# Second MLP layer as one product of 512 columns and one of 256, with channel 128 of the column DFT on GpSimd and two weight decodes moved

## The chip, the cores and the metric

The kernel runs on one core of a Trainium2 chip. The metric is device time in microseconds (us) of one execution. The text calls the engines TensorE (PE in the rows, PEld its weight loads), VectorE (DVE), ScalarE (ACT), GpSimd (POOL) and SyncE (SP), which issues the DMAs.

## The reference

The input is x, 2 x 3136 x 256 in float32. Three blocks follow one another.

```python
X = np.fft.rfft(x, axis=1)                       # spectral mixing
Yr = X.real @ w_r - X.imag @ w_i + b_r
Yi = X.real @ w_i + X.imag @ w_r + b_i
y = np.fft.irfft(soft_threshold(Yr, 0.01) + 1j * soft_threshold(Yi, 0.01), n=3136, axis=1)

xn = (y - mean) / sqrt(var + 1e-6) * g_ln        # MLP 1, weights in float64
z = y + np.maximum(xn @ w_ch1, 0) @ w_ch2        # 256 -> 1024 -> 256

u = z + np.real(np.fft.fft(np.fft.fft(z, axis=1), axis=2))
un = (u - mean) / sqrt(var + 1e-6)               # MLP 2, other weights in float64
out = u + np.maximum(un @ w_ch1, 0) @ w_ch2
```

## The kernel before, in words

**Stages.** The DFT over 3136 is done as 49 x 64 with matrices in two steps. Stages 1 to 3 are the mixing block, up to about 165 us. From there on the two MLPs fill the program: 13 chunks of MLP 1 (`mlp1[0]` to `mlp1[12]`), then 13 of MLP 2 (`mlp2[0]` to `mlp2[12]`), each chunk of up to four tiles of 128 rows. Stage 4 (`Stage98`) is the first step of the DFT over z. It is woven into MLP 1's chunks 7 to 10 for batch 0 and into MLP 2's chunks 0 to 3 for batch 1.

**Precision.** A matrix that needs more than one pass is held as two float32r parts, a high one (h) and a low one (l). A product is then three products: h by h, h by l, l by h. `mm3` (lines 214 to 216) and `mm3r` (lines 220 to 222) issue them.

**One MLP chunk.** `Chunk.prep` computes the layer norm, `Chunk.trans` transposes on TensorE (line 607) and splits into h and l (ScalarE line 612 or 202, VectorE line 613 or 210). `Chunk.l1` runs the first layer, eight slices `f` of 128 hidden units: six matmuls of 512 columns into a PSUM tile `psa` (three buffers), then ScalarE writes the ReLU's high part (line 631) and VectorE its low part (line 632), which frees `psa`. `Chunk.l2` runs the second layer tile by tile: 8 slices by three matmuls of 256 columns into `psb` (two buffers), then VectorE adds the residual `y` (line 649) and SyncE stores (line 657). There are 98 tiles in all, 49 for each MLP.

**Weights.** `load_mlp` brings each MLP's weights in eight pieces of float64 and VectorE decodes a piece to h and l in eight instructions (`decode64`, lines 506 to 514). They lie in `r3a` (MLP 1) and `r2b` (MLP 2), h and l in separate halves of the tile (`w_views`). `MLP2_AT` says after which slice of which MLP 1 chunk MLP 2's pieces are decoded.

**Stage 4.** For each group of two columns `Stage98.split` folds channel c with channel 256 - c on GpSimd (lines 360 to 362), ScalarE writes the high part `s` (line 202), GpSimd the low part (line 210), TensorE does three matmuls (`psc<-s`), ScalarE copies out (`o`), GpSimd puts channel 128 in (line 405), SyncE stores. Channel 128, which has no partner, goes apart: `middle` loads it for all columns (line 373, tile `m`), `middle2` splits it (`mhl`), multiplies it and copies it to `mid`.

**What sets the order.** Each engine takes its instructions in the order of the built program, and SyncE its DMAs. A scheduler makes that order: it lists what can run by a timeline of its own, so a change in one place moves instructions elsewhere. `tc.issue_after`, the tables above and buffer counts bind it.

Of the kernel before, what the change touches and what calls it, by code (L numbers as in the profile page):

```python
# [11 lines left out]
I32 = mybir.dt.int32  # L12
# [10 lines left out]
STAGE3_AT = (0,) * 16 + (3, 3, 3, 3, 3, 1)  # L23
CONST_AT = (0, 0, 1, 2, 2, 3, 4, 5, 6, 8)
MLP1_AT = (5, 8, 10, 12, 13, 14, 15, 18)
MLP2_AT = ((4, 6), (5, 2), (5, 6), (6, 2), (6, 6), (7, 3), (9, 3), (10, 6))
STAGE3_END = 3
STAGE3_MLP = ((0, 0), (0, 1), (0, 2), (0, 3), (1, 0), (1, 1), (1, 2), (1, 3),
              (2, 0), (2, 1), (2, 2), (2, 3), (3, 0))
# [18 lines left out]
ALU = mybir.AluOpType  # L48
# [5 lines left out]
D = 256  # L54
NQ = 98
# [5 lines left out]
NF = DFF // 128  # L61
# [101 lines left out]
def fourier_moe_kernel(ctx, tc, x, w_r, w_i, b_r, b_i, g_ln, w11, w12, w21, w22,  # L163
                       t_ca, t_cam, t_cim, t_cb, t_ci, t_cb0, t_ci0, t_cd, t_ident, out):
    nc = tc.nc
# [9 lines left out]
    def psum(tag):  # L175
        return pp.tile([128, 512], F32, tag="ps" + tag, name="ps" + tag, bufs=ps_bufs[tag])
# [20 lines left out]
    def oslot():  # L197
        return wk.tile([128, 4, D], F32, tag="o", name="o", bufs=2)


    def a_copy(o, i, scale=1.0):
        nc.scalar.activation(out=o, in_=i, func=AF.Copy, scale=scale)

    def v_copy(o, i):
        nc.vector.tensor_copy(o, i)
# [3 lines left out]
    def sub(eng, o, a, b):  # L209
        ins = eng.tensor_tensor(out=o, in0=a, in1=b, op=ALU.subtract)  # L210
        mark["pool" if eng is nc.gpsimd else "dve"] = getattr(ins, "ins", ins)

    def mm3(ps, lh, ll, rh, rl, first, last):
        nc.tensor.matmul(out=ps, lhsT=lh, rhs=rh, start=first, stop=False)  # L214
        nc.tensor.matmul(out=ps, lhsT=lh, rhs=rl, start=False, stop=False)  # L215
        nc.tensor.matmul(out=ps, lhsT=ll, rhs=rh, start=False, stop=last)  # L216
# [117 lines left out]
    class Stage98:  # L334
# [40 lines left out]

        def middle2(self):
            t, hl = self.mid_in
            v_copy(hl[:, 0], t)
            sub(nc.vector, hl[:, 1], t, hl[:, 0])
            ps = psum(self.tag)  # L380
            mm3(ps[0:NQ, 0:32], cs_h, cs_l, hl[:, 0], hl[:, 1], True, True)
            self.mid = wk.tile([NQ, 32], F32, tag="mid", name="mid", bufs=1)
            v_copy(self.mid, ps[0:NQ, 0:32])

        def start(self):
            self.middle()
# [106 lines left out]
    def load64(src3, tag):  # L493

        s64 = wk.tile([128, 512], I64, tag=tag, name="s64", bufs=2)
        o = s64 if len(src3.shape) == 2 else s64.rearrange("p (f c) -> p f c", f=src3.shape[1])
        sp.dma_start(out=o, in_=src3)
        return s64

    def decode64(s64, dh, dl, t1, t2):  # L500


        w, low = s64.bitcast(I32)[:, 1::2], s64.bitcast(U32)[:, 0::2]
        t1f, t2f = t1.bitcast(F32), t2.bitcast(F32)
        v = nc.vector
        v.tensor_scalar(out=t1, in0=w, scalar1=3, scalar2=0x3FFFF000,
                        op0=ALU.logical_shift_left, op1=ALU.bitwise_and)
        v.scalar_tensor_tensor(out=t1, in0=w, scalar=-0x40000000, in1=t1, op0=ALU.bitwise_and, op1=ALU.bitwise_or)
        v.tensor_scalar(out=t2, in0=w, scalar1=20, scalar2=0x7FF, op0=ALU.logical_shift_right, op1=ALU.bitwise_and)
        v.scalar_tensor_tensor(out=dh, in0=t2, scalar=896.0, in1=t1f, op0=ALU.is_gt, op1=ALU.mult)  # L510
        v.tensor_scalar(out=t2, in0=w, scalar1=0x1FF, scalar2=None, op0=ALU.bitwise_and)
        v.scalar_tensor_tensor(out=t2f, in0=low, scalar=2.0 ** -32, in1=t2, op0=ALU.mult, op1=ALU.add)
        v.tensor_scalar(out=t1, in0=dh.bitcast(I32), scalar1=-0x800000, scalar2=None, op0=ALU.bitwise_and)
        v.scalar_tensor_tensor(out=dl, in0=t2f, scalar=2.0 ** -20, in1=t1f, op0=ALU.mult, op1=ALU.mult)

    def load_mlp(w1, w2, r, tag, two):

        srcs, raw = [], {}  # L520
        for i in range(4):
            c, h = divmod(i, 2)
            srcs.append((w1[c * 128:(c + 1) * 128, h * 512:(h + 1) * 512], i * 512))
        for i in range(4):
            srcs.append((w2[i * 256:(i + 1) * 256, :].rearrange("(f p) c -> p f c", p=128), 2048 + i * 512))

        def ask(k):
            if k < 8 and k not in raw:
                raw[k] = load64(srcs[k][0], tag)

        def piece(k):
            def f():
                ask(k)
                if two:
                    ask(k + 1)
                    t1, t2 = (wk.tile([128, 512], I32, tag="t98", name="t64", bufs=TB) for _ in range(2))
                else:
                    t = wk.tile([128, 2, 512], I32, tag="stg", name="t64", bufs=SB)
                    t1, t2 = t[:, 0, :], t[:, 1, :]
                o = srcs[k][1]  # L540
                decode64(raw[k], r[:, 0, o:o + 512], r[:, 1, o:o + 512], t1, t2)
            return f

        return [lambda: ask(0)] + [piece(k) for k in range(8)]

    def w_views(r):
        return ([r[:, i, 0:2048].rearrange("p (k f) -> p k f", k=2) for i in range(2)],
                [r[:, i, 2048:].rearrange("p (f c) -> p f c", f=NF) for i in range(2)])

    class Chunk:  # L550

# [85 lines left out]
            self.h.append((h, l))  # L637

        def l2(self, i):
            _, (w2h, w2l) = self.wv  # L640
            if i == 0:
                self.o = oslot()
            ps = psum("b")
            ts_ = slice(i * 128, (i + 1) * 128)
            with tc.issue_after(self.last):
                for f in range(NF):
                    h, l = self.h[f]
                    mm3(ps[:, 0:D], h[:, ts_], l[:, ts_], w2h[:, f, :], w2l[:, f, :], f == 0, f == NF - 1)
            nc.vector.tensor_tensor(out=self.o[:, i, :], in0=ps[:, 0:D], in1=self.y[:, i, :], op=ALU.add)  # L649

        def store(self, last):

# [159 lines left out]

    r3 = cp.tile([128, 2, 4096], F32R, tag="r3", name="r3a")
    wv1 = w_views(r3)
    mlp1_w = load_mlp(w11, w12, r3, "o", False)[1:]
    todo = {}
# [84 lines left out]
    inv1 = lambda: inv[1].step()  # L901
    r2b = cp.tile([128, 2, 4096], F32R, tag="u1", name="r2b")
    wv2 = w_views(r2b)
    plan2 = [[((0, 4 * i + 2), (0, 4 * i + 1)), ((0, 4 * i + 4), (0, 4 * i + 3))] for i in range(6)]
    plan2 += [[((1, 2), (1, 1)), ((0, 0), (1, 0))]]
# [12 lines left out]
    def after(k, i, f):  # L918

        def g():  # L920
            with tc.issue_after(mlp1[k].rest[i]):
                f()
        return g
# [8 lines left out]
    def hook(k, part, i, f):  # L932
        hooks.setdefault((k, part, i), []).append(f)

    mlp2_w = load_mlp(w21, w22, r2b, "stg", True)
    hook(4, "l1", 2, mlp2_w[0])
    for (k, i), f in zip(MLP2_AT, mlp2_w[1:]):
        hook(k, "l1", i, after(k, i, f))
# [42 lines left out]
```

## Time and profile before

| what | value |
|---|---|
| runs | 838.01, 839.77, 841.67 us; median 839.77 |
| the profiled execution's own time | 835.99 us |
| its span, first to last instruction | 834.2 us |
| mean granted TensorE clock | 0.998 |
| busy share: TensorE, VectorE, ScalarE, GpSimd | 98%, 60%, 37%, 17% |
| DMA | 71.66 MB, mean 86 GB/s |

Busy shares are sums over the span. A matmul's duration in the rows includes its way through the array and overlaps the next one, so the pace of a stream of matmuls is read from the distance between starts, not from durations. In a row of the timeline, the brackets give the idle time of the engine just before it and what ended it.

### The profile page before, as it was taken

What the parts mean: (1) busy time and instruction counts of PE and PEld (TensorE: products, weight loads), DVE (VectorE), ACT (ScalarE), POOL (GpSimd) and SP (SyncE); (2) the same over time, 40 slices, a digit from 0 to 9 for tenths busy, and PEclk for the clock granted to TensorE, in tenths of its full rate; (3) what the DMA queues carried; (4) which work ended last, traced back from release to release, by engine and by line L of the source; (5) the groups of instructions that cost most, each with busy time, mean ns of one, the idle gap of its engine ahead of it and who ended that gap; (6) DMA issues with size and microseconds to landing.
All of it is one profiled execution on the core that took longest, in us unless ns stands there. A gap on an engine that the chain in (4) does not pass through costs nothing.

```text
span 834.2 us, 13615 instructions
## 1 busy us (share of the span) xinstructions
PE 813.7 (98%) x5240; PEld 716.1 (86%) x5240; DVE 499.3 (60%) x1152; ACT 312.3 (37%) x627; POOL 141.1 (17%) x198
## 2 busy tenths in 40 slices
PE   9999999999999999989999998999999999999997
PEld 3888977868888999959799998899899999999996
DVE  6579995475565578754755345625545566545652
ACT  1322356354343222364553225455532233322221
POOL 0212221320000000097410004345400000000000
PEclk9999999999999999999999999999999999999999
DMA  8642200711014321453133113343232122210001
GB/s 230 215 139 72 76 1 1 244 67 51 23 29 158 127 77 67 116 171 121 56 105 101 64 49 77 109 139 103 86 96 86 46 62 59 70 51 25 18 19 30
DMA packets 48180, 71.66 MB, mean 86 GB/s; under 512 B 11746, under 2 KB 32490, under 8 KB 47920
## 3 DMA queue, kind: packets, MB, share of 16 engines
q1 hardware_dynamic: 48116, 70.80, 27.6%
q8 instruction: 41, 0.67, 0.3%
q14 instruction: 23, 0.19, 0.1%
HBM read 45.09 MB, written 25.69 MB: 85 GB/s over the span
## 4 chain that ended last, share of the span: by engine, by line
PE 81%; DVE 8%; DMA 5%; SPq 2%; ACT 1%; POOL 1%; issue 1%; POOLq 0%; DVEq 0%; ACTq 0%
PE psb L215 11%; PE psb L216 11%; PE psb L214 11%; PE psa L220 10%; PE psa L221 9%; PE psa L222 9%; PE psb L461 4%; PE psc L320 3%; PE psc L708 2%; PE psc L607 2%; PE psc L301 2%; PE psc L481 1%; PE psa L429 1%; DMA h<-in_x_dram 1%; PE psa L733 1%; DVE h L632 1%
## 5 line engine op out<-in xcount | busy, mean ns | idle before, releaser
L631 ACT ACTIVATE h<-psa 128x512 fp32r<-128x512 f32 (+2 forms) x208 | 117.8, 573 | 260.5 <-PE psa L222 240.3
L632 DVE SCALAR_TENSOR_TENSOR h<-psa,h 128x512 fp32r<-128x512 f32 (+2 forms) x208 | 135.0, 654 | 101.0 <-ACT h L631 99.9
L214 PE MATMUL psb<-r2b,h 128*128 128x256 f32 x392 | 111.1, 286 | 0.0
L214 PE MATMUL psb<-r3a,h 128*128 128x256 f32 x392 | 110.1, 284 | 0.0
L215 PE MATMUL psb<-r2b,h 128*128 128x256 f32 x392 | 109.8, 283 | 0.0
L215 PE MATMUL psb<-r3a,h 128*128 128x256 f32 x392 | 109.7, 283 | 0.0
L216 PE MATMUL psb<-r3a,h 128*128 128x256 f32 x392 | 108.2, 283 | 0.0
L216 PE MATMUL psb<-r2b,h 128*128 128x256 f32 x392 | 107.5, 283 | 0.0
L649 DVE TENSOR_TENSOR o<-psb,yb 128x256 f32<-128x256 f32 x74 | 31.0, 424 | 101.8 <-PE psb L216 99.9
L461 PE MATMUL psb<-wm,h 128*128 128x256 f32 (+1 forms) x600 | 88.8, 298 | 1.1 <-DVE w L467 1.1
L220 PE MATMUL psa<-q,r3a 128*128 128x512 f32 (+2 forms) x208 | 83.8, 403 | 4.9 <-DVE h L632 4.8
L220 PE MATMUL psa<-q,r2b 128*128 128x512 f32 (+2 forms) x208 | 82.4, 396 | 3.4 <-DVE h L632 3.4
L461 PEld LDWEIGHTS psb<-wm,h 128*128 128x128 f32 (+1 forms) x600 | 76.1, 189 | 8.9 <-issue 8.3
L221 PE MATMUL psa<-q,r3a 128*128 128x512 f32 (+2 forms) x208 | 78.7, 379 | 0.0
L222 PE MATMUL psa<-q,r3a 128*128 128x512 f32 (+2 forms) x208 | 78.7, 381 | 0.0
L221 PE MATMUL psa<-q,r2b 128*128 128x512 f32 (+2 forms) x208 | 78.2, 378 | 0.0
L222 PE MATMUL psa<-q,r2b 128*128 128x512 f32 (+2 forms) x208 | 78.0, 379 | 0.0
L215 PEld LDWEIGHTS psb<-r3a,h 128*128 128x128 f32 x392 | 74.9, 192 | 1.0 <-issue 0.2
L214 PEld LDWEIGHTS psb<-r3a,h 128*128 128x128 f32 x392 | 74.8, 191 | 1.0 <-issue 0.3
L214 PEld LDWEIGHTS psb<-r2b,h 128*128 128x128 f32 x392 | 74.9, 191 | 0.7
L215 PEld LDWEIGHTS psb<-r2b,h 128*128 128x128 f32 x392 | 75.0, 192 | 0.5
L216 PEld LDWEIGHTS psb<-r3a,h 128*128 128x128 f32 x392 | 74.4, 191 | 0.3
(113 smaller groups left out, 1416.6 us busy)
## 6 DMA issues: line engine op xcount, KB each, us to landing
s<-in_moe_w_ch_dram SPq DMA_DIRECT2D x16, 512.0 KB
r<-dX SPq DMA_DIRECT2D x32, 196.0 KB
dA<-o SPq DMA_DIRECT2D x32, 196.0 KB
dY<-yg SPq DMA_DIRECT2D x12, 512.0 KB
r<-dA SPq DMA_DIRECT2D x48, 128.0 KB
dX<-o SPq DMA_DIRECT2D x11, 512.0 KB
yb<-dX SPq DMA_DIRECT2D x50, 64.0 KB
out_dram<-o SPq DMA_DIRECT2D x50, 64.0 KB
```

Of the source, the lines that this page charges most:

```text
L214: nc.tensor.matmul(out=ps, lhsT=lh, rhs=rh, start=first, stop=False)
L215: nc.tensor.matmul(out=ps, lhsT=lh, rhs=rl, start=False, stop=False)
L216: nc.tensor.matmul(out=ps, lhsT=ll, rhs=rh, start=False, stop=last)
L220: nc.tensor.matmul(out=ps, lhsT=lh, rhs=rh, start=first, stop=False)
L221: nc.tensor.matmul(out=ps, lhsT=ll, rhs=rh, start=False, stop=False)
L222: ins = nc.tensor.matmul(out=ps, lhsT=lh, rhs=rl, start=False, stop=last)
L301: nc.tensor.matmul(out=ps, lhsT=cam, rhs=self.raw[g // 2][:, e * 512:(e + 1) * 512], start=True, stop=True)
L320: nc.tensor.matmul(out=ps[0:NQ, :], lhsT=cim, rhs=t, start=True, stop=True)
L461: nc.tensor.matmul(out=ps[0:m, u * D:(u + 1) * D], lhsT=xv[:, o:o + m], rhs=wm_hl[wv][:, e, c, :], start=k == 0, stop=k == 11)
L631: nc.scalar.activation(out=h[:, 0:n], in_=ps[:, 0:n], func=AF.Relu)
L632: ins = nc.vector.scalar_tensor_tensor(out=l[:, 0:n], in0=ps[:, 0:n], scalar=0.0, in1=h[:, 0:n], op0=ALU.max, op1=ALU.subtract)
L649: nc.vector.tensor_tensor(out=self.o[:, i, :], in0=ps[:, 0:D], in1=self.y[:, i, :], op=ALU.add)
```

## The change

- The second layer issues two matmuls for each slice: the high hidden part by the weights' h and l side by side (512 columns, into all of `psb`), and the low hidden part by the weights' h (256 columns, into the first half). VectorE adds the first half and the residual, then the second half. For that, the second layer's weights are stored as h and l side by side for each slice, and `decode64` writes them there through views of two times 256 columns.
- `middle2`'s copy and subtraction go from VectorE to GpSimd, its copy out of PSUM from VectorE to ScalarE.
- MLP 2's pieces 6 and 7 are decoded in chunk 11 of MLP 1 (slices 2 and 6) and no longer in chunks 9 (slice 3) and 10 (slice 6).

```diff
-MLP2_AT = ((4, 6), (5, 2), (5, 6), (6, 2), (6, 6), (7, 3), (9, 3), (10, 6))
+MLP2_AT = ((4, 6), (5, 2), (5, 6), (6, 2), (6, 6), (7, 3), (11, 2), (11, 6))
...
         def middle2(self):
             t, hl = self.mid_in
-            v_copy(hl[:, 0], t)
-            sub(nc.vector, hl[:, 1], t, hl[:, 0])
+            nc.gpsimd.tensor_copy(hl[:, 0], t)
+            sub(nc.gpsimd, hl[:, 1], t, hl[:, 0])
...
-            v_copy(self.mid, ps[0:NQ, 0:32])
+            a_copy(self.mid, ps[0:NQ, 0:32])
...
-                decode64(raw[k], r[:, 0, o:o + 512], r[:, 1, o:o + 512], t1, t2)
+                if k < 4:
+                    v = r.rearrange("p h f -> p (h f)")
+                    decode64(raw[k], v[:, o:o + 512], v[:, 2048 + o:2560 + o], t1, t2)
+                else:
+                    v = w_views(r)[1][:, 2 * k - 8:2 * k - 6, :]
+                    decode64(raw[k], v[:, :, 0:D], v[:, :, D:2 * D], t1, t2)
...
-                    mm3(ps[:, 0:D], h[:, ts_], l[:, ts_], w2h[:, f, :], w2l[:, f, :], f == 0, f == NF - 1)
-            nc.vector.tensor_tensor(out=self.o[:, i, :], in0=ps[:, 0:D], in1=self.y[:, i, :], op=ALU.add)
+                    nc.tensor.matmul(out=ps, lhsT=h[:, ts_], rhs=w2[:, f, :], start=f == 0, stop=False)
+                    nc.tensor.matmul(out=ps[:, 0:D], lhsT=l[:, ts_], rhs=w2[:, f, 0:D], start=False, stop=f == NF - 1)
+
+            o = self.o[:, i, :]
+            nc.vector.tensor_tensor(out=o, in0=ps[:, 0:D], in1=self.y[:, i, :], op=ALU.add)
+            nc.vector.tensor_tensor(out=o, in0=ps[:, D:2 * D], in1=o, op=ALU.add)
```

Line numbers shift with the change: the layers' matmuls are at lines 220 to 222 as before and at 658 and 659, the transposes (607) at 617, lines 612 and 613 at 622 and 623, 631 and 632 at 641 and 642, and the adds (649) at 662 and 663.

**TensorE, where chunk 0 of MLP 2 ends its second tile** (`psb` the tile's sum, `h` the hidden slice, `mhl` channel 128 of batch 1). Before:

```order
L214 MATMUL psb_5192<-r2b_1656,h_5102 128x256
L215 MATMUL psb_5192<-r2b_1656,h_5102 128x256
L216 MATMUL psb_5192<-r2b_1656,h_5102 128x256
L214 MATMUL psc_5249<-mhl_5174,ca_hl_73 98x32
L215 MATMUL psc_5249<-mhl_5174,ca_hl_73 98x32
L216 MATMUL psc_5249<-mhl_5174,ca_hl_73 98x32
```

With the change:

```order
L658 MATMUL psb_4842<-r2b_1656,h_4759 128x512
L214 MATMUL psc_4885<-mhl_4824,ca_hl_73 98x32
L659 MATMUL psb_4802<-r2b_1656,h_4759 128x256
L659 MATMUL psb_4842<-r2b_1656,h_4759 128x256
L215 MATMUL psc_4885<-mhl_4824,ca_hl_73 98x32
L216 MATMUL psc_4885<-mhl_4824,ca_hl_73 98x32
```

Three matmuls of a slice have become two, the columns are the same, and channel 128's products stand at the tile's end as before.

**VectorE, at the first layer of the same chunk** (`h<-psa` the hidden slices' low parts, `m` channel 128 as loaded). Before:

```order
L649 TENSOR_TENSOR o<-psb,yb 128x256 x2
L632 SCALAR_TENSOR_TENSOR h<-psa,h 128x512 x2
L205 CAST mhl<-m_5173 98x32
L632 SCALAR_TENSOR_TENSOR h<-psa,h 128x512
L210 TENSOR_TENSOR mhl<-m_5173,mhl 98x32
L205 COPY w<-psa 128x2
```

With the change:

```order
L662 TENSOR_TENSOR o<-psb,yb 128x256
L663 TENSOR_TENSOR o<-psb,o 128x256
L642 SCALAR_TENSOR_TENSOR h<-psa,h 128x512 x3
L205 COPY w<-psa 128x2
L642 SCALAR_TENSOR_TENSOR h<-psa,h 128x512
L205 COPY w<-w 128x1
```

The two instructions that need `m` have left VectorE's queue, and each tile has two adds.

**ScalarE, at the start of stage 4, chunks 7 and 8 of MLP 1** (`s` the folded columns' high part, `q<-psc` the transposed rows' high part, which chunk 8's first layer reads). Before:

```order
L593 ACTIVATE q<-q,sm 128x256 x2
L631 ACTIVATE h<-psa 128x256 x3
L612 ACTIVATE q<-psc,g_sb 128x512 x2
L631 ACTIVATE h<-psa 128x256
L202 ACTIVATE s_1657<-w 98x512 x4
L631 ACTIVATE h<-psa 128x512 x3
```

With the change:

```order
L603 ACTIVATE q<-q,sm 128x256 x4
L202 ACTIVATE s_1657<-w 98x512
L622 ACTIVATE q<-psc,g_sb 128x512
L202 ACTIVATE s_1657<-w 98x512
L622 ACTIVATE q<-psc,g_sb 128x512
L202 ACTIVATE mid<-psc 98x32
L202 ACTIVATE s_1657<-w 98x512 x2
L641 ACTIVATE h<-psa 128x512 x3
```

The two `q` copies stood ahead of all `s` copies; now each has an `s` copy ahead of it.

## Rows read from the trace of the kernel before

**Rows 1.** Page: busy time by engine, and the chain that ended last.

```profile
PE 813.7 (98%) x5240; PEld 716.1 (86%) x5240; DVE 499.3 (60%) x1152; ACT 312.3 (37%) x627; POOL 141.1 (17%) x198
...
PE 81%; DVE 8%; DMA 5%; SPq 2%; ACT 1%; POOL 1%; issue 1%; POOLq 0%; DVEq 0%; ACTq 0%
```

**Rows 2.** Timeline, TensorE: 48 matmuls of 256 columns (start us, us, engine, line, ...).

```profile
510.09 0.28 PE L214 MATMUL psb<-r2b,h 128*128 128x256 f32 x1
...
515.72 0.28 PE L216 MATMUL psb<-r2b,h 128*128 128x256 f32 x1
515.85 0.18 PE L214 MATMUL psc<-mhl,ca_hl 98*98 98x32 f32 x1
```

**Rows 3.** Timeline, TensorE: two streams of 512 columns, 8 and 11 starts.

```profile
397.30 0.39 PE L220 MATMUL psa<-q,r3a 128*128 128x512 f32 x1
...
399.11 0.39 PE L222 MATMUL psa<-q,r3a 128*128 128x512 f32 x1
...
504.31 0.40 PE L221 MATMUL psa<-q,r2b 128*128 128x512 f32 x1
...
506.87 0.61 PE L733 MATMUL psa<-cd,w 128*128 128x129 f32 x4
```

**Rows 4.** Chain of waits, its pieces (start us, us, what): transposes of 128 columns.

```profile
488.37 0.66 PE psc L607 x6
```

**Rows 5.** Timeline, chunk 0 of MLP 2: the load of channel 128.

```profile
498.05 0.91 SPq L373 DMA_DIRECT2D m<-dX  x1
503.14 0.18 DVE L205 CAST mhl<-m 98x32 fp32r<-98x32 f32 x1 [4.19 <-DMA m<-dX]
503.97 0.50 PE L220 MATMUL psa<-q,r2b 128*128 128x512 f32 x1 [2.35 <-DVE h L632]
```

**Rows 6.** Timeline, chunk 9: the decode there, and its first wide step in chunk 10.

```profile
400.68 1.23 DVE L508 SCALAR_TENSOR_TENSOR t<-s,t 128x512 int32<-128x512 int32 x1
401.95 1.79 DVE L510 SCALAR_TENSOR_TENSOR r2b<-t,t 128x512 fp32r<-128x512 int32 x1
404.39 0.50 PE L220 MATMUL psa<-q,r3a 128*128 128x512 f32 x1 [1.57 <-DVE h L632]
433.50 0.68 DVE L508 SCALAR_TENSOR_TENSOR t<-s,t 128x512 int32<-128x512 int32 x1
```

**Rows 7.** Windows (us, busy us and instructions by engine, clock, DMA): two stretches.

```profile
300.00:320.00 20.00, 20.00 (x139) 18.73 (x138) 16.70 (x36) 5.16 (x11) 0.00 (x0) 1.00 0.18 56
410.00:500.00 90.00, 90.00 (x594) 81.97 (x594) 45.22 (x113) 28.48 (x57) 2.27 (x6) 1.00 0.24 76
```

**Rows 8.** Timeline, start of stage 4 on all engines.

```profile
344.19 0.42 DVE L649 TENSOR_TENSOR o<-psb,yb 128x256 f32<-128x256 f32 x1 [0.56 <-PE psb L216]
353.08 0.85 POOL L360 TENSOR_TENSOR w<-r 98x254 f32<-98x254 f32 x1 [165.16 <-DMA r<-dX]
355.33 0.63 ACT L202 ACTIVATE s<-w 98x512 fp32r<-98x512 f32 x1 [5.79 <-POOL w L362]
360.24 5.02 POOL L210 TENSOR_TENSOR s<-w,s 98x512 fp32r<-98x512 f32 x4
361.56 0.47 PE L222 MATMUL psc<-s,ca_hl 98*98 98x512 f32 x1 [0.76 <-POOL s L210]
371.06 0.51 PE L220 MATMUL psa<-q,r3a 128*128 128x512 f32 x1 [2.56 <-DVE h L632]
```

**Rows 9.** Timeline, VectorE: channel 128's load in chunk 7, and two adds back to back.

```profile
351.83 0.18 DVE L205 CAST mhl<-m 98x32 fp32r<-98x32 f32 x1 [2.54 <-DMA m<-dX]
356.46 0.74 DVE L649 TENSOR_TENSOR o<-psb,yb 128x256 f32<-128x256 f32 x2
```

**Rows 10.** Waits: VectorE's add for TensorE (us in total, times, longest).

```profile
DVE o L649 <- PE psb L216: 124.8, 84, 4.1
```

More of the change, by code (lines that the diff above doesn't have):

```diff
@@ L500, in decode64, with cut @@
     def decode64(s64, dh, dl, t1, t2):
+        def cut(a):
+            return a if len(dh.shape) == 2 else a.rearrange("p (f c) -> p f c", f=dh.shape[1])
         w, low = s64.bitcast(I32)[:, 1::2], s64.bitcast(U32)[:, 0::2]
@@ L509, in decode64 @@
         v.tensor_scalar(out=t2, in0=w, scalar1=20, scalar2=0x7FF, op0=ALU.logical_shift_right, op1=ALU.bitwise_and)
-        v.scalar_tensor_tensor(out=dh, in0=t2, scalar=896.0, in1=t1f, op0=ALU.is_gt, op1=ALU.mult)
+        v.scalar_tensor_tensor(out=dh, in0=cut(t2), scalar=896.0, in1=cut(t1f), op0=ALU.is_gt, op1=ALU.mult)
         v.tensor_scalar(out=t2, in0=w, scalar1=0x1FF, scalar2=None, op0=ALU.bitwise_and)
         v.scalar_tensor_tensor(out=t2f, in0=low, scalar=2.0 ** -32, in1=t2, op0=ALU.mult, op1=ALU.add)
-        v.tensor_scalar(out=t1, in0=dh.bitcast(I32), scalar1=-0x800000, scalar2=None, op0=ALU.bitwise_and)
-        v.scalar_tensor_tensor(out=dl, in0=t2f, scalar=2.0 ** -20, in1=t1f, op0=ALU.mult, op1=ALU.mult)
+        v.tensor_scalar(out=cut(t1), in0=dh.bitcast(I32), scalar1=-0x800000, scalar2=None, op0=ALU.bitwise_and)
+        v.scalar_tensor_tensor(out=dl, in0=cut(t2f), scalar=2.0 ** -20, in1=cut(t1f), op0=ALU.mult, op1=ALU.mult)
     def load_mlp(w1, w2, r, tag, two):
@@ L546, in w_views @@
     def w_views(r):
-        return ([r[:, i, 0:2048].rearrange("p (k f) -> p k f", k=2) for i in range(2)],
-                [r[:, i, 2048:].rearrange("p (f c) -> p f c", f=NF) for i in range(2)])
+        v = r.rearrange("p h f -> p (h f)")
+        return ([v[:, i * 2048:(i + 1) * 2048].rearrange("p (k f) -> p k f", k=2) for i in range(2)],
+                v[:, 4096:].rearrange("p (f c) -> p f c", f=NF))
     class Chunk:
@@ L639, in l2 @@
         def l2(self, i):
-            _, (w2h, w2l) = self.wv
+            _, w2 = self.wv
             if i == 0:
```

## Prediction

> **What bounds the kernel now.** I read the page first: TensorE is busy 98% of the span, and 81% of the chain that ended last is TensorE's [rows 1]. What shortens its stream or fills its few idle stretches shortens the kernel; work that other engines gain or lose costs only where TensorE comes to wait for it. Then the timeline of TensorE for the pace of its matmuls, from start to start. In the second layer, 48 matmuls of 256 columns start within 515.85 - 510.09 = 5.76 us, 120 ns each [rows 2]. In the first layer, 8 of 512 columns take 399.11 - 397.30 = 1.81 us, 226 ns each, and 11 take 506.87 - 504.31 = 2.56 us, 233 ns each [rows 3]. Twice 120 is 240, so a matmul of 512 columns is cheaper than two of 256: some 11 ns are paid per matmul, not per column. Last, the timeline's brackets, for where TensorE is idle: 2.35 us behind the load of channel 128 [rows 5], 1.57 us behind a decode [rows 6], and several stretches where stage 4 starts [rows 8].
>
> **The second layer's matmuls.** The change keeps the columns (768 for each slice) and makes two matmuls of three. There are 98 tiles of 8 slices, 784 slices. Before, a slice takes 3 x 120 = 360 ns. Now it takes one matmul of 512 and one of 256 columns. I price the wide one at 229 ns, the middle of 226 and 233 [rows 3], and leave the other at 120 [rows 2]: 349 ns, 11 less. 784 x 11 ns = 8.6 us. By the two ends it is 14 ns or 11.0 us, and 7 ns or 5.5 us. The weight loads are as wide as before and one fewer. A load of 128 columns hides behind a matmul of 256 already: transposes with half those columns come every 110 ns [rows 4], and a 256-column matmul with its load takes only 120.
> The page "TensorE: Matmul & The Clock Gate" of the Trainium skill, section "Back-to-back issue gap", gives columns / 2.4 GHz + 2.5 ns between starts. By that only 2.5 ns would be fixed, and 784 of them are an estimate of 2.0 us. The rows disagree (120 and 226 to 233 ns, where it gives 109 and 216), so the rows' 11 ns stand.
>
> **The second add.** VectorE gets 98 more adds. Two back to back take 0.74 us [rows 9], so each adds 0.74 - 0.42 = 0.32 us, 31 us in all. They lie beside TensorE's next tile (8 x 349 ns = 2.8 us), and VectorE was idle before 84 of the 98 old adds, 124.8 us in all, for want of TensorE [rows 10]. Behind an add stand the next chunk's low parts, which free `psa`, and `psb` comes free 0.32 us later with a tile of 2.8 us in between. I take nothing on the path, except after the last tile, where nothing follows: +0.3 us. Without the cover it is up to +31 us.
>
> **Channel 128.** In chunk 0 of MLP 2, VectorE waits 4.19 us for the load, with a low part queued behind it, and TensorE waits 2.35 us for `psa` [rows 5]. In the change the two instructions stand on GpSimd, ahead of the first folds, and VectorE's low parts follow each other. GpSimd's folds could not start earlier anyway: the columns come after channel 128 in the DMA queue (load seen at 351.83, first fold at 353.08 in the first half [rows 8, 9]). The cast took 0.18 us on VectorE; on GpSimd I take two of some 0.2 to 0.7 us, which fit into those 1.25 us. TensorE needs the product only at the second tile's end, some 10 us after the load. ScalarE's copy to `mid` stands behind `s` copies that need GpSimd anyway; I take nothing. What is late next is `psa` by the ReLUs, as in the other chunks. I take -2.35 us; the bounds are -2.35 and 0. In the first half VectorE's 2.54 us [rows 9] lie beside second-layer matmuls and cost nothing now.
>
> **The decode out of chunk 9.** There the steps stretch to 1.23 and 1.79 us while GpSimd works, against 0.68 in chunk 10, and TensorE waits 1.57 us for the low part queued behind them [rows 6]. I take -1.57 us, bounds -1.57 and 0. In chunk 11, two decodes meet: 16 instructions, some 9 us of VectorE, beside 8 x 0.6 us of low parts and one chunk of TensorE, 22 us. GpSimd is nearly idle there (2.27 us from 410 to 500 us), and a stretch with two decodes already exists: from 300 to 320 us VectorE is busy 16.70 us and TensorE 20.00 of 20 [rows 7]. I take nothing. The decode's new output views hold the same elements; hidden as the decode was.
>
> **The start of stage 4, chunks 7 and 8.** Here the scheduler's new order bears on the path. Chunk 8's transposes now come late in chunk 7's second layer, and on ScalarE each of the two `q` copies that chunk 8 reads has an `s` copy ahead of it. Count from VectorE's add at 344.19, which lets the store and then the loads go. The first fold started 8.9 us later, and the `s` copy 11.1 us later [rows 8]. With the second add ahead of the store, 11.5; then 0.63 for it and some 0.7 for the `q` copy: TensorE may start chunk 8 at +12.8. It will be through with chunk 7 at about +9.4 (24 x 120 ns, 8 x 110 ns and 16 x 349 ns from the add): a wait of 3.4 us. Then the products with `s` need GpSimd's low parts, which follow four folds (353.08 to 360.24, 7.2 us) and take 5.02 / 4 each: the third at 9.2 + 7.2 + 3.8 = +20.2, where TensorE, 27 matmuls of 230 ns on, stands at +19: 1.5 us with what it waits for the others. That is 4.9 us, in place of idle stretches that are now 0.76 and 2.56 us. The difference, 1.6 us, is no larger than what the count leaves out (a restart after each stretch, transposes that now stand ahead). I take 0, with -2 and +3 as bounds.
>
> **The sum.** -8.6 + 0.3 - 2.35 - 1.57 + 0 = -12.2 us. It is made against the profiled execution, 835.99 us, which becomes 823.8. That one was 3.8 us below the median of the runs, 839.77; a difference carries over, so I forecast 839.77 - 12.2 = 827.6 us.
>
> **Rivals.**
> *Only the matmuls count.* The idle stretches come back elsewhere: in chunk 11 behind two decodes, in chunk 0 of MLP 2 behind the ReLUs, since an order made anew has new short waits. For it: the scheduler moved much. Against it: where neither GpSimd nor a load held VectorE up, TensorE ran 90.00 of 90 us [rows 7]. -8.6 + 0.3 gives 831.5 us. Chance 0.24.
> *Stage 4 starts later.* The folds come 3 us later than worked out, by loads that other DMAs slow down; all of it is TensorE's wait, as chunk 8's `q` copies stand behind. -12.2 + 3 gives 830.6. Chance 0.07.
> *VectorE sets the pace.* The one on the other side: the adds push the first layer's low parts back, and TensorE waits for `psa`. The price is 0.32 us wherever VectorE has no idle time before the add. With all 98 it is +31 - 12.2, 858.6 us; it passes no change when over 38 of 98 tiles pay (12.2 / 0.32). Only 14 had no wait [rows 10], and in the busiest stretch VectorE has 3.3 us free in 20 us, against some four adds or 1.3 us [rows 7]. Chance 0.05.
> *The change does little of what it is for:* beside the hidden part's loads the wide matmul costs 237 ns, as far above 233 as 233 is above the middle, and 3 ns for each slice or 2.4 us are saved instead of 8.6. No row shows 237 [rows 3]: 839.77 - 2.4 + 0.3 - 3.9 = 833.8. Chance 0.06. The Trainium skill's formula above would give about the same.
> *Weight loads are on the path.* Then each of 784 loads gives back up to the 110 ns between transposes [rows 4], 86 us: 839.77 - 86 - 3.6 = 750 us. Against it: three loads and three matmuls in 360 ns [rows 2] leave no room for loads by themselves. Chance 0.02. The same page of the Trainium skill, section "What overlaps and what doesn't", says that a load overlaps running matmuls only when it goes to another row group, which these full ones do not; the trace disagrees by those 120 ns.
> The forecast itself has 0.56.
>
> **How the numbers follow.** The forecast's own range takes the ends of the matmuls' price (-11.0 to -5.5) and of stage 4 (-2 to +3): 823 to 834. A median of three runs moves by 2 us either way (838.01 to 841.67). From 820 to 835 all but the last rival and VectorE at its worst lie inside. A measurement tells about 0.5% from no change, 4.2 us: faster means below 835.6. Faster: nearly all of the forecast (0.54), most of the first rival (0.20) and of the second (0.05), half of the fourth, all of the last: 0.85. Slower: most of VectorE's case, 0.05. The rest is 0.10.
>
> **What would show it.** The two matmuls of a slice should start 120 and 226 to 233 ns apart from their successors, 2.8 us a tile; if not, the first term falls. TensorE's busy time should drop by about 9 us. No wait of VectorE for `m`, no idle TensorE near chunk 0 of MLP 2, none by a decode in chunks 9 or 11. Chunk 8 should begin with a wait of some 3 us behind ScalarE's `q` copy; 6 or more would be the second rival. Waits of TensorE for VectorE's line 642 that sum to over 12 us would make the forecast wrong outright, as would matmuls of 512 columns at 240 ns.

## The result, and the profile after

The changed kernel takes 831.05 us (median of 4 runs, 830.75 to 831.76) against 839.71 us before (4 runs, 838.01 to 841.67): a ratio of 0.9897, 95% interval 0.9875 to 0.992, so 1.03% or 8.7 us faster. A second set of runs gave 830.96 us and a ratio of 0.991 (0.9885 to 0.9934). My forecast was 827.6 us with a range of 820 to 835. The time lies inside the range, 3.4 us above the forecast, but the sum behind the forecast was wrong in several of its terms.

The page of the profiled execution (831.31 us), its busy line and its chain by engine, and then the cores view:

```profile
span 829.5 us, 12209 instructions
...
PE 810.0 (98%) x4456; PEld 676.6 (82%) x4456; DVE 533.4 (64%) x1244; ACT 313.5 (38%) x629; POOL 139.9 (17%) x202
...
PE 79%; DVE 9%; DMA 5%; ACT 2%; SPq 2%; issue 1%; POOL 1%; POOLq 0%; ACTq 0%
```

```profile
core 0: 829.5 us, clock 0.995
```

784 matmuls fewer, as worked out, and TensorE still bounds the kernel. VectorE took on 34 us. But TensorE's busy time fell by 3.7 us only [rows 1], where I had expected some 9. First the pace, in chunk 10 (timeline of TensorE after the change: start us, us, instruction):

```profile
419.74 0.40 PE L658 MATMUL psb<-r3a,h 128*128 128x512 f32 x1
419.98 0.28 PE L659 MATMUL psb<-r3a,h 128*128 128x256 f32 x1
420.09 0.40 PE L658 MATMUL psb<-r3a,h 128*128 128x512 f32 x1
420.33 0.28 PE L659 MATMUL psb<-r3a,h 128*128 128x256 f32 x1
420.45 0.40 PE L658 MATMUL psb<-r3a,h 128*128 128x512 f32 x1
...
421.51 0.40 PE L658 MATMUL psb<-r3a,h 128*128 128x512 f32 x1
```

Five slices take 421.51 - 419.74 = 1.77 us, 354 ns each; over the whole trace the medians are 233 ns from a wide matmul to the next start and 117 from a narrow one, 350 ns, where 360 was the pace before [rows 2]. 784 x 10 ns is 7.8 us, near the forecast 8.6. Not every start lies at the median, though: summed from start to start over the whole trace, the second layer takes 277.8 us where it took 283.6, so 5.8 us less. The waits of TensorE sum to 12.1 us where they summed to 14.1. Against that, the first layer without its waits takes 282.4 us where it took 280.5, as TensorE's clock falls where stage 4 is. Windows of 5 us after the change (us; busy us and instructions of PE, PEld, DVE, ACT, POOL; granted clock, DMA share, GB/s):

```profile
355.00:360.00 5.00, 4.50 (x13) 3.43 (x14) 2.16 (x4) 3.02 (x6) 5.00 (x10) 0.66 0.79 219
...
395.00:400.00 5.00, 3.91 (x12) 3.04 (x13) 2.64 (x5) 5.00 (x12) 2.01 (x3) 0.72 0.47 152
400.00:405.00 5.00, 5.00 (x26) 4.04 (x25) 2.23 (x4) 3.88 (x7) 1.63 (x3) 0.94 0.39 138
```

In the profile of before the same three windows have a granted clock of 1.00, the first two of them here:

```profile
355.00:360.00 5.00, 5.00 (x25) 4.00 (x25) 2.27 (x5) 1.90 (x3) 5.00 (x9) 1.00 0.41 123
395.00:400.00 5.00, 4.90 (x22) 3.66 (x21) 4.20 (x12) 4.86 (x12) 5.00 (x10) 1.00 0.26 79
```

Now the drop at 355 and the one from 395 on each follow an idle stretch of TensorE, and the matmuls run for a while at the lower of the two levels, 1.2 GHz. Timeline of TensorE where chunk 8 starts:

```profile
355.50 0.50 PE L220 MATMUL psa<-q,r3a 128*128 128x512 f32 x1 [2.66 <-ACT q L622]
...
357.22 0.63 PE L221 MATMUL psa<-q,r3a 128*128 128x512 f32 x1
357.65 0.63 PE L222 MATMUL psa<-q,r3a 128*128 128x512 f32 x1
358.08 0.63 PE L220 MATMUL psc<-s,ca_hl 98*98 98x512 f32 x1
```

357.22, 357.65, 358.08: starts lie some 430 ns apart instead of 230. Seven such starts cost 7 x 0.2 = 1.4 us on top of the 2.66. Chunk 9 has the same pair (timeline: VectorE, ScalarE, TensorE):

```profile
388.34 0.36 DVE L588 BATCH_NORM_AGGREGATE mv<-st 128x2 f32<-128x6 f32 x4
388.74 4.35 DVE L599 TENSOR_SCALAR ng<-mv 128x4 f32<-128x4 f32 x1
...
393.13 1.71 ACT L602 ACTIVATE q<-yb,ng 128x256 f32<-128x256 f32 x4 [4.09 <-DVE ng L599]
...
396.09 0.50 PE L220 MATMUL psa<-q,r3a 128*128 128x512 f32 x1 [1.80 <-DVE h L642]
```

The decode that stretched there [rows 6] is gone. But the negation of the means, 128x4 and 0.16 us at its shortest, now holds VectorE for 4.35 us; ScalarE's normalisation waits for it, the ReLUs stand behind that, and TensorE waits 1.80 us, with some 1.5 us of half-clock starts after it. GpSimd's rows over that time, back to back up to the pause of 3.20 us:

```profile
388.58 0.78 POOL L360 TENSOR_TENSOR w<-r 98x254 f32<-98x254 f32 x1
389.27 0.78 POOL L361 TENSOR_TENSOR w<-r 98x254 f32<-98x254 f32 x1
...
392.28 0.79 POOL L361 TENSOR_TENSOR w<-r 98x254 f32<-98x254 f32 x1
392.96 0.24 POOL L362 COPY w<-r 98x4 f32<-98x4 f32 x1
396.40 1.30 POOL L210 TENSOR_TENSOR s<-w,s 98x512 fp32r<-98x512 f32 x1 [3.20 <-ACT s L202]
```

VectorE's instruction ends at 388.74 + 4.35 = 393.09, as GpSimd's third pair of folds ends (392.28 + 0.79 = 393.07).

In chunk 0 of MLP 2, VectorE no longer waits for channel 128 and TensorE's 2.35 us [rows 5] are gone. What came instead is smaller (timeline; SyncE's queue, GpSimd, ScalarE, TensorE):

```profile
500.58 0.92 SPq L373 DMA_DIRECT2D m<-dX  x1
...
504.75 0.24 POOL L378 CAST mhl<-m 98x32 fp32r<-98x32 f32 x1 [73.52 <-DMA m<-dX]
...
507.70 0.63 ACT L202 ACTIVATE s<-w 98x512 fp32r<-98x512 f32 x1 [2.90 <-POOL w L362]
508.24 0.58 ACT L641 ACTIVATE h<-psa 128x512 fp32r<-128x512 f32 x1
...
513.17 1.96 PE L617 MATMUL psc<-ident,q 128*128 128x128 f32 x8 [1.06 <-ACT q L603]
```

ScalarE now stands 2.90 us at an `s` copy with a ReLU and the layer norm queued behind it, and TensorE waits 1.06 us for the norm.

### The profile page after: what moved, and what is told of

It is laid out like the page before. It is cut to its first block, busy times and chain, and to the rows that moved or that the text cites. A ratio compares the mean times of both kernels' runs of the same rounds, so it can differ in the third digit from the quotient of the medians.

```text
span 829.5 us, 12209 instructions
## 1 busy us (share of the span) xinstructions
PE 810.0 (98%) x4456; PEld 676.6 (82%) x4456; DVE 533.4 (64%) x1244; ACT 313.5 (38%) x629; POOL 139.9 (17%) x202
## 4 chain that ended last, share of the span: by engine, by line
PE 79%; DVE 9%; DMA 5%; ACT 2%; SPq 2%; issue 1%; POOL 1%; POOLq 0%; ACTq 0%
PE psb L658 20%; PE psa L220 11%; PE psb L659 10%; PE psa L221 10%; PE psa L222 10%; PE psb L461 3%; PE psc L320 3%; PE psc L722 3%; PE psc L617 2%; PE psa L429 1%; PE psc L481 1%; DMA h<-in_x_dram 1%; PE psc L301 1%; DVE h L642 1%; DMA r<-dX 1%
## 5 line engine op out<-in xcount | busy, mean ns | idle before, releaser
L658 PE MATMUL psb<-r2b,h 128*128 128x512 f32 x392 | 137.6, 399 | 0.0
L658 PE MATMUL psb<-r3a,h 128*128 128x512 f32 x392 | 137.3, 399 | 0.0
L659 PE MATMUL psb<-r3a,h 128*128 128x256 f32 x392 | 106.1, 282 | 0.0
L659 PE MATMUL psb<-r2b,h 128*128 128x256 f32 x392 | 105.5, 280 | 0.0
L658 PEld LDWEIGHTS psb<-r3a,h 128*128 128x128 f32 x392 | 71.6, 188 | 15.6 <-PE psa L222 0.3
L658 PEld LDWEIGHTS psb<-r2b,h 128*128 128x128 f32 x392 | 71.9, 188 | 14.9
L659 PEld LDWEIGHTS psb<-r3a,h 128*128 128x128 f32 x392 | 73.7, 189 | 4.1 <-issue 1.0
L659 PEld LDWEIGHTS psb<-r2b,h 128*128 128x128 f32 x392 | 73.9, 189 | 3.0
L202 ACT ACTIVATE yg<-psc 98x512 f32<-98x512 f32 (+2 forms) x58 | 48.4, 860 | 55.0 <-PE psc L320 26.7
L210 POOL TENSOR_TENSOR h<-w 128x512 f32<-128x512 f32 (+1 forms) x26 | 34.5, 1328 | 109.1 <-DVE w L468 61.5
L220 PEld LDWEIGHTS psa<-q,r3a 128*128 128x128 f32 x208 | 39.7, 191 | 15.8 <-DVE h L642 5.0
```

The lines of the kernel that those rows point to most:

```text
L658: nc.tensor.matmul(out=ps, lhsT=h[:, ts_], rhs=w2[:, f, :], start=f == 0, stop=False)
L659: nc.tensor.matmul(out=ps[:, 0:D], lhsT=l[:, ts_], rhs=w2[:, f, 0:D], start=False, stop=f == NF - 1)
```

## The experiments

Each is set against the kernel before on the same chip (838.99, 839.09 and 838.86 us in the three sets of four). Intervals are 95% intervals of the ratio.

**The second layer alone.** The kernel before with the new second layer, its weights' layout and its two adds; `middle2` and `MLP2_AT` unchanged.

> Kernel before with the second layer's edit alone (one matmul of 512 columns and one of 256 per slice, two adds); channel 128 on VectorE and the decodes where they were. Theory (the whole gain is the matmuls' pace: 784 slices x 10 ns = 7.8 us, less 0.3 for the last add; the other two edits give nothing): 831 to 833 us, within 1.5 us of the full change. Rival (the other edits gave part of the 8.7 us): 834 us or more. Rival (the other edits cost, so the matmuls gave more): under 829.5.

Measured: 835.47 us (832.50 to 840.55), ratio 0.9962 (0.9939 to 0.9985): 3.5 us, not 7.8. VectorE and TensorE on its timeline, then two windows:

```profile
504.18 0.18 DVE L205 CAST mhl<-m 98x32 fp32r<-98x32 f32 x1 [6.87 <-DMA m<-dX]
...
505.31 0.79 PE L220 MATMUL psa<-q,r2b 128*128 128x512 f32 x1 [5.32 <-DVE w L205]
```

```profile
500.00:505.00 5.00, 0.00 (x0) 0.00 (x0) 0.78 (x4) 0.31 (x2) 0.00 (x0) 0.99 0.55 67
505.00:510.00 5.00, 4.69 (x16) 3.86 (x17) 4.79 (x15) 1.82 (x6) 3.48 (x6) 0.67 0.20 56
```

With channel 128 still on VectorE, the order made for the new second layer puts VectorE at that load earlier: it waits 6.87 us where it waited 4.19 [rows 5], TensorE does nothing from 500 to 505 us and then runs at a granted clock of 0.67. The wait alone grew by 3.0 us. The changed kernel's two new waits are here too, with the decodes where they were: 2.68 us for `q` at chunk 8's start, and 2.01 us behind the held negation in chunk 9, where TensorE no longer waits for the decode (VectorE, then TensorE):

```profile
388.97 4.57 DVE L599 TENSOR_SCALAR ng<-mv 128x4 f32<-128x4 f32 x1
396.54 0.50 PE L220 MATMUL psa<-q,r3a 128*128 128x512 f32 x1 [2.01 <-DVE h L642]
```

So these waits come with the second layer's edit. My theory that the matmuls gave all of the gain falls. But the 3.5 us are net of the waits and not the price of the matmuls by themselves.

**Channel 128 alone.**

```diff
-            v_copy(hl[:, 0], t)
-            sub(nc.vector, hl[:, 1], t, hl[:, 0])
+            nc.gpsimd.tensor_copy(hl[:, 0], t)
+            sub(nc.gpsimd, hl[:, 1], t, hl[:, 0])
...
-            v_copy(self.mid, ps[0:NQ, 0:32])
+            a_copy(self.mid, ps[0:NQ, 0:32])
```

> Kernel before with channel 128's split on GpSimd and its copy on ScalarE alone. Theory (VectorE's wait for m goes, but ScalarE's s copies now stand ahead of ReLUs and TensorE waits for those instead): 839 to 841 us, no gain, an idle stretch of 1 to 2.5 us still there within 10 us of the second channel 128. My prediction's term: 2.35 us less, 837.4, no idle TensorE there.

Measured: 834.46 us (833.97 to 837.31), ratio 0.995 (0.9931 to 0.997): 4.5 us (2.5 to 5.8 by the interval), more than my term of 2.35 and its bound, and against the theory. TensorE is busy 5.00 of 5 us from 500 to 505, where it was idle for 2.35; nothing came in the wait's place:

```profile
500.00:505.00 5.00, 5.00 (x27) 4.15 (x26) 3.50 (x10) 2.15 (x6) 0.55 (x2) 1.00 0.65 97
```

**The decodes alone** (`MLP2_AT` with 11, 2 and 11, 6 in place of 9, 3 and 10, 6).

> Kernel before with the two decodes moved from chunks 9 and 10 to chunk 11 alone. Theory (another small VectorE operation is stretched by GpSimd's folds in chunk 9, and TensorE waits for what is queued behind it): 839 to 841 us, a VectorE operation on 128x4 that takes over 1 us in chunk 9 and a wait of TensorE behind it. My prediction's term: 1.57 us less, 838.1, and no wait in chunk 9.

Measured: 837.39 us (835.10 to 840.45), ratio 0.9979 (0.9962 to 0.9996): 1.6 us, my term. The negation is stretched here too, to 1.19 us at 396.04, but TensorE does not wait behind it: its longest wait in chunk 9 is 0.11 us. So my theory falls for this edit by itself; holds of over 4 us come with the order that the second layer's edit makes.

The three edits by themselves give 3.5 + 4.5 + 1.6 = 9.6 us, together 8.1 to 8.7: about a sum. That is no proof that they are independent: the wait that channel 128's edit takes away is 3.0 us longer in the first of the three kernels than in the kernel before, and the wait that the decodes' move takes away is not in it.

**Three matmuls again.** The changed kernel with the wide matmul split in 7 of 8 slices:

```diff
-                    nc.tensor.matmul(out=ps, lhsT=h[:, ts_], rhs=w2[:, f, :], start=f == 0, stop=False)
+                    if f == 0:
+                        nc.tensor.matmul(out=ps, lhsT=h[:, ts_], rhs=w2[:, f, :], start=True, stop=False)
+                    else:
+                        nc.tensor.matmul(out=ps[:, D:2 * D], lhsT=h[:, ts_], rhs=w2[:, f, D:2 * D], start=False, stop=False)
+                        nc.tensor.matmul(out=ps[:, 0:D], lhsT=h[:, ts_], rhs=w2[:, f, 0:D], start=False, stop=False)
```

> Changed kernel with the 512-column matmul split into two of 256 again in 7 of 8 slices (the first slice of a tile stays wide); both adds, the weights' layout and all else as in the change. Theory (the pace per matmul is the gain): 686 slices x 10 ns = 6.9 us more than the change, 837 to 839 us. Rival (the new order of the instructions or the removed waits are the gain): 831 to 833 us.

Measured: 833.95 us, ratio 0.9938 (0.9917 to 0.9958), 3 us more than the change, between theory and rival. The pace is back at 120 ns, and the sum of the second layer's starts is 283.1 us against 277.8 in the change, 5.3 more. But TensorE's waits sum to 10.3 us where the change has 12.1: at chunk 8's start the change waits 2.66 us for `q`, this kernel 0.54 us for `s`. The quicker TensorE comes earlier to what stage 4 delivers, and waits there.

**The change again, and three ways to take a wait away.** On one chip:

> The changed kernel itself, unedited, beside the three kernels that follow on one chip: 831 us, granted clock 0.993 to 0.996 in its runs, a narrower spread than the kernel before (whose runs lie between 835 and 844 us, longer the lower the granted clock). If its spread is as wide as that of the kernel before, the theory that the wait for channel 128 made the spread falls.

830.96 us (828.56 to 833.14), 4.6 us wide in 6 runs where the kernel before is 5.1 us wide in 17: so the theory that channel 128 makes the spread falls. (With channel 128's edit alone it was 3.3 us in 10 runs, against 8.2 in 27 of the kernel before; the changed kernel has new idle stretches elsewhere.) In the runs of the kernel before the time goes with the granted clock (below); in these six it does not clearly: 831.50 us at 0.998, 830.24 at 0.994.

The negation of the means on ScalarE:

```diff
-                nc.vector.tensor_scalar(out=ng[:, 0:nt], in0=mv[:, 0:nt, 0], scalar1=-1.0, scalar2=None, op0=ALU.mult)
+                nc.scalar.activation(out=ng[:, 0:nt], in_=mv[:, 0:nt, 0], func=AF.Copy, scale=-1.0)
```

> Changed kernel with the negated means of the layer norm (128x4) computed on ScalarE instead of VectorE, nothing else. Theory (this small VectorE operation, held 4.35 us while GpSimd folds, is what makes ScalarE's ReLU and TensorE late in chunk 9): the 1.80 us wait of TensorE near 396 us and the half-clock matmuls behind it go, 2 to 3.5 us less than the change, 827.5 to 829. Rival (another VectorE operation is held in its place): within 1 us of the change.

830.01 us (826.83 to 835.61), ratio 0.9902 (0.987 to 0.9934): no difference from the change that this can tell. The wait in chunk 9 is gone and the negation takes 0.25 us at most. The view of line 599 (shortest, median and longest in ns; first and last start) in this kernel, then in the change:

```profile
L599 ACT ACTIVATE ng<-mv x8: 188/192/248, 341.6 to 598.9; 128x4 f32<-128x4 f32 x8
```

```profile
L599 DVE TENSOR_SCALAR ng<-mv x8: 155/696/4354, 341.7 to 597.5; 128x4 f32<-128x4 f32 x8
```

But chunk 8's start now waits 3.17 us, and 18 us later TensorE waits 1.90 us more, where the next small operation of VectorE is held in turn (line 594, 2.80 us at 370.30). Mechanism as expected, time as the rival had it.

ScalarE's first two `s` copies behind the `q` copies of chunk 8 (`with tc.issue_after(mlp1[8].qc): a_copy(h, f)`, and stage 4 begun one tile later):

> Changed kernel with ScalarE's first two s copies of stage 4 ordered behind the two q copies that chunk 8 reads, nothing else asked. Theory (ScalarE's queue order makes the 2.66 us wait at chunk 8's start, and the half-clock stretch behind it): both go, up to 4 us less than the change, 827 to 829. Rival (the products with s then come late and TensorE waits for GpSimd's low parts instead): 830 to 832.

831.87 us, ratio 0.9919 (0.9894 to 0.9943): the rival. The `q` wait is gone and four others stand in its place (timeline of TensorE):

```profile
363.22 0.47 PE L222 MATMUL psc<-s,ca_hl 98*98 98x512 f32 x1 [1.35 <-POOL s L210]
...
364.46 0.48 PE L222 MATMUL psc<-s,ca_hl 98*98 98x512 f32 x1 [0.76 <-POOL s L210]
...
365.69 0.74 PE L222 MATMUL psc<-s,ca_hl 98*98 98x512 f32 x1 [0.76 <-POOL s L210]
...
377.41 0.50 PE L220 MATMUL psa<-q,r3a 128*128 128x512 f32 x1 [3.14 <-DVE h L647]
```

The `s` copies of the second stage 4 behind the layer norm of chunk 1 of MLP 2 (the same, with the norm's last instruction):

> Changed kernel with ScalarE's first two s copies of the second stage 4 ordered behind the layer norm of chunk 1 of MLP 2, nothing else asked. Theory (the 2.90 us that ScalarE stands at an s copy, with ReLU and layer norm behind it, makes the 1.06 us wait of TensorE and the slowed transposes at 513 us): 1 to 2.3 us less than the change, 829 to 830. Rival (stage 4's products come late instead): no change or slower.

835.73 us, ratio 0.9967 (0.9946 to 0.9988): 4.8 us slower than the change. A copy still stands ahead of the norm and waits longer; VectorE stands at the norm's reciprocal with a tile's adds behind it, and `psb` comes free late (ScalarE, VectorE, TensorE):

```profile
511.86 0.63 ACT L202 ACTIVATE s<-w 98x512 fp32r<-98x512 f32 x1 [6.06 <-POOL w L362]
...
512.71 0.18 DVE L596 RECIPROCAL sm<-sm 128x4 f32<-128x4 f32 x1 [5.64 <-ACT sm L595]
...
514.17 0.74 DVE L667 TENSOR_TENSOR o<-psb,yb 128x256 f32<-128x256 f32 x2
...
515.39 0.52 PE L663 MATMUL psb<-r2b,h 128*128 128x512 f32 x1 [4.46 <-DVE o L668]
```

**A third add.** The first add issued twice for each tile.

> Changed kernel with the first of the two adds done twice for every tile: 98 more VectorE operations of 0.3 to 0.4 us, some 31 us of VectorE. Theory (VectorE's adds lie beside TensorE's next tile): 830 to 834 us, VectorE's busy time up by some 30 us, TensorE's waits nearly unchanged. Rival from my prediction (VectorE sets the pace): up to 31 us more, 862; anything over 838 speaks for it.

843.76 us (840.55 to 848.16), ratio 1.0063 (1.0039 to 1.0087): 12.8 us more than the change in the set before, for 34.4 us of VectorE (567.8 against 533.4). It lies over 838 us, which I had set as the mark of the rival, at 37% of the adds' length: VectorE's adds are covered only up to a point. It shows in the middle chunks, where nothing of stage 4 runs yet; the change first, then this kernel:

```profile
270.00:290.00 20.00, 20.00 (x104) 16.97 (x103) 13.14 (x35) 6.25 (x11) 0.00 (x0) 1.00 0.22 83
290.00:310.00 20.00, 20.00 (x104) 17.00 (x103) 16.48 (x42) 4.89 (x10) 0.00 (x0) 1.00 0.13 53
```

```profile
270.00:290.00 20.00, 19.46 (x98) 16.00 (x98) 14.74 (x40) 6.37 (x11) 0.00 (x0) 1.00 0.36 118
290.00:310.00 20.00, 19.35 (x101) 15.82 (x100) 14.07 (x34) 4.37 (x8) 0.00 (x0) 1.00 0.13 52
```

With two adds TensorE is busy 20.00 of 20 us there; with three it loses 0.5 to 0.7 us in every 20.

**The negation with two operands**, on VectorE (`scalar_tensor_tensor`, means times -2 plus the means).

> Changed kernel with the negated means (128x4) still on VectorE, as an operation of two operands (means times -2, plus the means) in place of one of a single operand. Theory (it is this form of operation that GpSimd's folds hold up): it takes under 1 us in chunk 9, TensorE does not wait there, as with the negation on ScalarE: 829 to 831 us. Rival (any VectorE operation that meets back-to-back folds is held until they pause): it takes 4 us or more again, and TensorE waits 1.8 to 2.8 us near 395 us.

831.41 us, ratio 0.9912 (0.9885 to 0.9939). The rival: this form is held as the other was, and TensorE waits 2.03 us for what stands behind it.

```profile
390.87 4.59 DVE L599 SCALAR_TENSOR_TENSOR ng<-mv 128x4 f32<-128x4 f32 x1
```

**Two attempts at a better kernel.** First the negation on ScalarE, and the `s` copies of the second stage 4 behind the last ReLU of chunk 0:

> Changed kernel with the negated means on ScalarE and, in the second stage 4, ScalarE's first two s copies behind the last ReLU of chunk 0 of MLP 2. Theory (ScalarE's stand of 2.9 to 3.3 us at the s copy makes the wait of 1.1 to 1.5 us at 513 us): 1 to 1.5 us less than with the negation alone, 828 to 829.5. Rival (the products with s come late instead, as when the copies stood behind the layer norm): 831 or more.

831.86 us, ratio 0.9917 (0.989 to 0.9943). The rival: TensorE waits 1.63 us for GpSimd's low part at 507.32 and still 1.60 us for the norm at 509.39.

Then also the first stage 4 later, from chunk 8's last `l1` slice on:

> The kernel with both edits of the run before, and in the first stage 4 ScalarE's first s copies behind chunk 8's q copies and its products from the end of chunk 8's first layer on, in program order on TensorE. Theory (chunk 8's start then waits for nothing of stage 4, and the products find their low parts ready): the 2.5 to 3.2 us wait at 355 us and the half-clock stretch behind it go with nothing in their place, 824 to 827 us. Rival (a wait turns up where the products now stand, or the later steps crowd chunks 9 and 10): 829 or more.

832.20 us, ratio 0.9924 (0.9902 to 0.9947). The wait at chunk 8's start falls to 0.55 us, and another turns up 8 us later:

```profile
352.43 0.50 PE L221 MATMUL psa<-q,r3a 128*128 128x512 f32 x1 [0.55 <-ACT q L630]
...
360.38 0.79 PE L221 MATMUL psa<-q,r3a 128*128 128x512 f32 x1 [3.53 <-DVE h L652]
```

ScalarE's four `s` copies, each waiting some 0.9 us for GpSimd, stand ahead of three ReLUs. No version beat the change.

## Why the prediction was right, and where not

**The second layer's matmuls (-8.6 forecast).** The median pace came as worked out: 350 ns a slice where I had 349, 7.8 us over 784. Summed over the trace it is 5.8 us, a third less than the term, because some starts come later than the rows I priced from. The larger error is in the sum, which took TensorE's pace for the kernel's. Alone the edit gave 3.5 us, with the longer wait for channel 128 as the largest loss (5.32 us against 2.35); put back into the changed kernel, three matmuls cost 3 us. By the formula on the Trainium skill's page "TensorE: Matmul & The Clock Gate", section "Back-to-back issue gap", which the page gives for the isolated matmul, a matmul less saves 2.5 ns. The rows show 10 in the median and 7 in the sum, so the rows were the better price.

**The second add (+0.3).** In the chunks away from stage 4 it is hidden, by 20.00 of 20 us busy. Of the rival *VectorE sets the pace* the mechanism exists, one add further on: 98 more cost 12.8 us, under 40% of their length, not the 100% that I put as its price. What the second add costs near stage 4 was not measured by itself.

**Channel 128 (-2.35, bounds -2.35 and 0).** Measured 4.5 us. The step that failed is the bound: I took the idle stretch of one execution as the most that could come back. That execution was one of the shortest, 835.99 us against a median of 839.77, with a granted clock of 0.998. And I wrote that "a difference carries over" to the median. It does not: of the 57 runs of the kernel before beside these experiments, the 9 with a granted clock of 0.998 or more took 836.9 us on average, and the 20 with 0.993 or less took 840.5. The runs at the median lose time to the lower clock that the profile did not show. That taking an idle stretch away spares them such losses fits the larger gain: granted clocks were 0.994 to 0.999 with this edit alone, 0.990 to 0.998 without, and 0.988 to 0.995 with the second layer's edit alone, where the stretch is 5.32 us. At equal clock the term comes out near its size: a straight line through the 57 runs falls by 0.62 us for each 0.001 of granted clock, and the runs with this edit alone lie 2.9 us below it on average. From profile to profile the edit gave 835.99 - 833.97 = 2.0 us. That is an argument from the clock of runs, not an experiment on it. From profile to profile the whole change gave 835.99 - 831.31 = 4.7 us, from median to median 8.7. So it is partly luck that the time lies in the range: against the execution that the sum was made for, the sum was 7.5 us too large, and 3.8 of these came back because that execution was a short one of its kernel, while the changed kernel's was a typical one.

**The decodes (-1.57).** Measured 1.6 us alone (0.3 to 3.2 by the interval), and TensorE's wait in chunk 9 went. In the whole change there is another: 1.80 us behind the held negation, and half-clock matmuls after it. As the second layer's edit brings that wait and leaves none for the decode, it is open whether the move gives anything in the changed kernel.

**The start of stage 4 (0, bounds -2 and +3).** The wait for ScalarE's `q` copy that I worked out at 3.4 us is there at 2.66, and 2.48 to 3.17 in the other profiles that start stage 4 in this order. I set it against the stretches it replaces. I missed the clock after it, 1.4 us, and the held negation of chunk 9. The two new waits, 2.66 and 1.80 us, with 1.4 and 1.5 us of half-clock starts behind them make 7.4 us.

**The rivals.** *Only the matmuls count* named 831.5 us, almost the time measured. Its mechanism was half right: idle stretches did come back elsewhere, in chunk 0 of MLP 2 behind ScalarE's queue, though not in chunk 11. But its sum was not: alone, the matmuls gave 3.5 us and not 8.3, and the other two edits about 6. The time fits by sums that cancel. *Stage 4 starts later*: the first fold comes 352.67 - 343.82 = 8.85 us after the add, no later than before. *The change does little of what it is for*: the second layer gave 5.8 us on TensorE, not 2.4. *Weight loads are on the path*: excluded by 350 ns a slice.

## What to carry to other kernels

Where one engine is 98% busy, a quicker pace on it is worth its full price only where the other engines keep up: price the waits that the quicker engine will run into, stage by stage. Read the times of many runs before one profile, and ask whether the profiled execution is a typical one; if the granted clock varies from run to run, an idle stretch may cost more than its length. An order that a scheduler makes anew moves waits as readily as it removes them: of six attempts to take a wait out of the changed kernel, none shortened it measurably.

## What the runs showed of the hardware

A small VectorE operation can be held over a run of GpSimd instructions that follow each other without a pause. The 128x4 negation, 0.16 us at its shortest, took 4.35, 5.38 and 4.59 us in three profiles (the change, the change again, two operands), and ended each time within 0.03 us of the end of a GpSimd fold (393.09 beside 393.07 in the change). The Trainium skill's page "SBUF — State Buffer", section "SBUF: two separate sides", says that VectorE and GpSimd share a port pair as an exclusive lock, held for a whole instruction while the other is fully blocked, where VectorE's operation is in a 2-port mode or has two inputs in SBUF. The ends agree with a lock that is let go between instructions. The length goes beyond it: the hold spanned some eight GpSimd instructions in a row, so VectorE did not get its turn after the first. It is not always so: with the decodes moved alone, the negation ended after 1.19 us and GpSimd went straight on. What decides this is open. That this port is the cause was not tested; only the place of the negation and its form were, and the form made no difference.

TensorE came back at half clock after idle stretches of 2.66, 1.80 and 5.32 us, yet at full clock after 2.56 and 2.35 us in the profiled run of the kernel before [rows 8, 5]. In the profile of the two-operand negation, whose order is nearly that of the change, it waits 2.79 us until 358.17 and 2.03 us until 398.46, and the windows behind both show full clock:

```profile
360.00:365.00 5.00, 4.43 (x20) 3.10 (x18) 2.01 (x6) 3.10 (x6) 5.00 (x6) 1.00 0.75 257
400.00:405.00 5.00, 5.00 (x27) 4.10 (x26) 2.08 (x4) 5.00 (x11) 1.68 (x4) 1.00 0.78 283
```

So the length of the stretch alone does not decide it in these rows.
